# An own PSUM tile for product six's seed in the first block of units of an FNet and FFN kernel, and some 300 pieces in another order

## The chip, the cores and the metric

The kernel runs on one core of a Trainium2 chip. The metric is the device time of one execution in microseconds (us). The kernel before took 670.1 us (median of three runs, 669.82 to 670.17).

## What is computed

A Fourier mixing layer with a residual, then a feed-forward layer with a residual, on 2048 rows of 512 numbers:

```python
def _A_ref(x, dft_seq_re, dft_seq_im, dft_hid_re, dft_hid_im):
    a = jnp.einsum("bsd,ed->bse", x, dft_hid_re)
    b = jnp.einsum("bsd,ed->bse", x, dft_hid_im)
    return jnp.einsum("ts,bse->bte", dft_seq_re, a) - jnp.einsum("ts,bse->bte", dft_seq_im, b)
...
def _B_ref(x, w1, w2):
    return silu(x @ w1) @ w2          # w1 512 x 1792, w2 1792 x 512
...
h = x + _A_ref(_layernorm(x), ...)
h2 = h + _B_ref(_layernorm(h), w1, w2)
```

## The kernel before

**Matmuls.** Every number that goes into a matmul is split in two parts, a rounded one (names that end in `h`) and the remainder (names that end in `l`). ScalarE (ACT) writes the rounded part, VectorE (DVE) the remainder: for most pieces these are the lines L265 and L269 (L271 where the sign changes), with the parts called `ph` and `pl`. One product of two such pieces is three matmuls on TensorE (PE), written by `three` at L313 to L317: rounded by rounded (L315), weight's rounded part by the other's remainder (L316), and weight's remainder by the other's rounded part (L317). So a matmul on L316 is the first that needs a new `pl`.

**Stages.** The rows are cut in two halves, q = 0 and q = 1. The order on PE is: `plain(0, 0)`, `fast(1, 0)`, `mix_fast(0)` (the Fourier layer for the first half of the columns of the spectrum), `fast(0, 1)`, `fast(1, 1)`, `mix_fast(1)` (the other half), then `up(0)` with the first part of `down(0)` inside it, the rest of `down(0)`, `up(1)` with the first part of `down(1)` inside, and the rest of `down(1)`. `fast`, `mix_fast`, `up` and `down` form block products by seven products in place of eight, so that sums and differences of blocks have to be made on DVE (L713 sums of DFT blocks `raw`, L834 sums of `c` and `h` blocks, L1141 to L1144 sums of the blocks `u` and `v` of w2, L1154 remainders of these, `Ul` and `Vl`). `h` blocks with the residual are made by L834 from the banks `y` that `mix_fast(1)` leaves.

**`up`.** `up(q)` multiplies the normed rows, as seven blocks T1 to T7, by w1. The hidden units come in seven blocks of 256, p = 0 to 6. The products of a block have numbers. For p = 0 they stand in the order 1, 7, 6, 2, 5; for the others in the order 1, 7, 3 (of the block ahead), 6, 2, 4 (of the block ahead), 5. Each product is six matmuls of 128x512. Three PSUM buffers of a block collect them: Y takes the products 1, 6, 5 and 3, V takes 7 and 4, and X takes 2. X doesn't start at zero but with product one: after it, `post(1)` has ACT copy Y to X at L1082. This copy is called the seed here. Product six goes on adding into Y, so it must wait until the seed has read product one out of Y. That is the seed of the title.

**Tiles.** PSUM is a pool of four tiles of two banks each (`banks`, L259). `mm` at L1061 takes a tile for Y at product one, and at product seven a tile whose first bank is V and whose second bank is X (L1065, L1066). A wait is set between whole tiles: an instruction that writes a tile waits for the last instructions that wrote or read that tile, on either bank. The names in the profile are those of the tiles: `y` for Y, `vx` for V and X.

**What sets the order.** `program` doesn't issue anything at once. It makes a list of events, each with a time in us, a class and a function: `step` (L321) makes the matmuls of a product, what has to be ready ahead of them (so long ahead) and what follows (so long behind). At the end the list is sorted by time plus `MOVED[number]` (table at L48 to L155: a number of us by which an event is moved). The launch replays the sorted list, and `issue_after` keeps each engine's instructions in that order. So the order of each of the five queues (PE, DVE, ACT, GpSimd as POOL, SyncE as SP) comes from these times. The same sorted list also sets which of 51 SBUF pages every block gets (`Plan`), and so which earlier reader a write to a page waits for. A seed's event stands at the end of product one plus `SEED_US`, 0.05 (L1127 in `up`), and since the events of product seven have the time of that end, the seed is recorded behind product seven.

Of the kernel before, what the change touches and what calls it, by code (L numbers as in the profile page):

```python
# [51 lines left out]
    31: -141.11, 32: -134, 33: -264.77, 34: -169.45, 35: -126.48, 36: -103.37, 37: -217.84, 38: -155.57, 39: -94.89,  # L52
    40: -79.42, 41: -142.14, 42: -135.16, 44: -117.87, 45: -98.55, 46: -92.57, 48: -183.29, 49: -129.46, 50: -108.53,
    52: -98.47, 53: -97.74, 54: -16.55, 56: -4.92, 57: -23.81, 58: -8.89, 59: -147.46, 60: -133.99, 61: -101.4,
    62: -14.81, 63: -139.64, 64: -134.82, 65: -9.83, 66: -7.55, 67: -130.2, 68: -99.62, 69: -129.85, 71: -159.25,
    72: -134.4, 73: -167.67, 74: -112.4, 75: -90, 76: -8.28, 78: -130.86, 79: -106.36, 80: -186.23, 81: -152.86,
    82: -111.9, 84: -114.65, 85: -104.21, 86: -113.16, 87: -95.06, 88: -11.303, 89: -19.86, 92: -21.38, 93: -18.33,
    94: -129.79, 95: -106.07, 96: -6.71, 97: 1.06, 98: -97.01, 99: -91.41, 100: -17.37, 102: -27.59, 103: -16.9,
    104: -102.24, 106: -1.27, 107: -9.08, 108: -204.21, 109: -106.59, 110: -253.17, 111: -121.9, 112: -39.16,
    114: -2.55, 115: 0.78, 116: 3.06, 118: -49.98, 119: -21.09, 121: -8.78, 122: -3.61, 123: 2.24, 125: 1.31,  # L60
    126: -17.83, 127: -3.73, 129: 0.38, 130: 1.11, 132: -7.91, 133: 0.36, 135: 0.25, 136: -1.05, 138: -3.38,
    139: -40.3, 140: -33.76, 142: -9.61, 143: -11.31, 145: -2.69, 146: -10.66, 147: -10.63, 148: -8.83, 149: -7.82,
    150: -3.56, 151: -28.92, 152: 0.89, 153: 5.11, 154: 28.43, 155: 25.79, 156: -19.1, 157: 11.48, 158: 12.64,
    159: 23.23, 160: 21.61, 161: -6.36, 162: -4.7, 163: -3.36, 164: 0.29, 165: -2.68, 166: -0.5, 167: -0.32,
    168: -3.05, 169: -6.02, 170: -7.36, 171: -16.72, 172: -14.58, 173: -1.38, 174: -3.55, 175: -6.71, 176: -1.18,
    177: 6.42, 178: 2.55, 179: 3.85, 180: 2.57, 181: -55.12, 182: -141.38, 183: -35.06, 184: -35.03, 185: -33.65,
    186: -22.94, 187: -27.65, 188: -24.62, 189: -15.8, 190: -18.21, 191: -20.38, 192: -17.85, 193: -18.3, 194: -16.61,
    195: -16.49, 196: -37.35, 197: -39.52, 198: -8.42, 199: -16.79, 200: -18.96, 201: -10.89, 202: -33.77,
    203: -23.77, 204: -6.04, 205: -22.6, 206: -26.07, 207: -19.3, 208: -13.56, 209: -11.57, 210: -2.02, 211: -14.92,
    212: -13.44, 213: -2.69, 214: -12.02, 215: -4.58, 216: -5.05, 217: -7.76, 218: -5.18, 219: 4.31, 220: -26.78,  # L70
    221: -14.68, 222: 2.53, 223: -1.3, 224: 9.8, 225: 9.6, 226: -4.61, 227: -6.71, 228: 7.13, 229: -6.57, 230: 4.19,
    231: 2.3, 233: -17.54, 234: -3.28, 235: -2.51, 237: -5.35, 238: 3.96, 239: 1.79, 241: -16.85, 242: -8.31,
    243: -10.48, 245: 2.48, 246: -6.71, 247: 5.57, 248: 4.96, 250: -7.84, 251: 4.88, 252: 7.47, 254: -3.03,
    255: -1.83, 256: -3.76, 258: -3.74, 259: -1.52, 260: 0.28, 262: 14.24, 263: -3.6, 264: 6.12, 265: 4.15,
    267: -1.21, 268: 1.61, 269: 1.26, 271: -12.23, 272: 6.33, 273: 4.4, 275: 6.84, 276: 3.77, 277: 4.66, 279: 8.32,
    280: 2.16, 281: 3.8, 282: -2.2, 283: -3.37, 284: 3.13, 285: -5.36, 287: 2.19, 288: 7.38, 290: 1.75, 291: 0.99,
    293: 7.28, 294: 5.11, 295: -0.57, 296: 2.29, 297: 1.12, 298: -6.11, 300: 6.15, 301: 5.36, 302: 6.99, 304: 0.33,
    305: 0.04, 307: 4.4, 308: 5.67, 310: 6.65, 311: 6.52, 312: 4.54, 313: 6.14, 314: 6.33, 315: 2.16, 317: 4.42,
    318: 5.39, 319: 6.85, 321: -1.92, 322: 0.78, 324: 7.21, 325: 5.83, 327: 5.44, 328: 3.63, 329: 5.68, 330: 5.23,
    331: 4.54, 332: 3.57, 335: 5.77, 336: 6.96, 337: 7.55, 339: 1.8, 340: 7.4, 343: 1.08, 344: 2.71, 347: 5.46,  # L80
    348: 7.81, 349: 7.74, 352: -11.6, 353: -5.61, 354: 0.23, 355: 7.05, 356: 4.21, 359: 4.35, 362: 0.73, 363: 3.66,
    364: -18.86, 366: 2.5, 367: 4.06, 371: -3.02, 372: 2.17, 374: 11.59, 376: 2.43, 377: 2.49, 380: 4.33, 381: 19.37,
    382: 4.31, 383: 5.86, 385: 0.07, 391: 3, 392: 5.29, 393: 4.78, 394: 5.84, 396: -6.06, 398: 3.97, 399: 5.33,
    402: 4.7, 403: 2.54, 404: 1.44, 407: 4.06, 408: 4.25, 411: 3.24, 412: 3.09, 413: 4.05, 414: 5.92, 417: 5.6,
    418: 6.69, 420: 16.42, 422: 4.72, 423: 5.68, 424: 0.95, 425: 4.17, 428: 5.12, 429: 3.15, 430: -5.26, 432: 13.47,
    433: 30.5, 434: -12.86, 435: -18.34, 436: -20.06, 437: -17.24, 438: -20.28, 439: -14.87, 440: -17.12, 441: -18.08,
    442: -8.62, 443: -3.41, 444: 6.22, 445: 4.67, 446: 4.65, 447: 3.36, 448: -30.45, 449: -29.1, 450: -35.51,
    451: -21.41, 452: -16.94, 453: -18.24, 454: -12.602, 455: -15.99, 456: -8.99, 457: -10.56, 458: 1.51, 459: -5.57,
# [1300 lines left out]
```

## Time and profile before

| | before |
|---|---|
| median of three runs | 670.1 us (669.82 to 670.17) |
| the profiled execution's own time | 670.99 us |
| its span, first to last instruction | 669.2 us |
| granted TensorE clock, mean | 0.999 |
| PE busy | 659.8 us, 99% |
| DVE busy | 578.3 us, 86% |
| ACT busy | 369.5 us, 55% |
| POOL busy | 97.1 us, 15% |
| DMA, mean of the span | 275 GB/s |

Times in the profile are us from the first instruction. A row of the timeline has the start, the duration, the engine, the line, the operation, what it writes and reads, and in square brackets how long the engine sat idle ahead of it and what released it. `PEld` rows are weight loads, which run beside matmuls. A matmul's recorded duration is 0.39 us, but they are pipelined: in a row of matmuls without a wait one starts about 0.227 us behind the other. A DVE operation also overlaps the next a little: 128x1024 takes 1.22 us in its row, and the next starts 1.13 to 1.14 us behind it.

### The profile page before, as it was taken

To read this page: it belongs to the slowest core of one execution; us is meant where nothing else is said; L and a number is where in the kernel's file an instruction comes from. 1 tells how busy PE (TensorE), PEld (TensorE's weight loads), DVE (VectorE), ACT (ScalarE), POOL (GpSimd) and SP (SyncE) were. 2 spreads that over 40 slices of the span, in tenths; PEclk is the share of its full clock that TensorE was granted. 3 is DMA by queue.
4 is the path that set the end of the run, shared out by engine and by line. 5 is a ranking of instruction groups with operands and counts; after the bars stand their busy time and mean duration, and the time that the engine had idled before them with its cause. 6 is when DMAs were issued, how large, how long until landed. Compare 5 with 4: busy or idle time off the path is not lost. (4 is left out here: it accounts for less than half of the span.)

```text
span 669.2 us, 8292 instructions
## 1 busy us (share of the span) xinstructions
PE 659.8 (99%) x2892; PEld 541.6 (81%) x2892; DVE 578.3 (86%) x727; ACT 369.5 (55%) x476; POOL 97.1 (15%) x128
## 2 busy tenths in 40 slices
PE   9999999999999999999999999999999999999997
PEld 5888888888888888887878878888888788888885
DVE  7999978998989989989999998989998854369964
ACT  6996546754465336455656445778544555664600
POOL 0011011112002523211120015243000000000000
PEclk9999999999999999999999999999999999999999
DMA  8973899798996768999999993859989635278803
GB/s 316 375 190 81 263 332 417 233 329 262 385 361 259 242 215 198 389 296 377 359 332 414 334 401 120 328 214 321 343 278 361 232 116 221 79 248 310 322 31 127
DMA packets 59706, 184.22 MB, mean 275 GB/s; under 512 B 6800, under 2 KB 13840, under 8 KB 59664
## 3 DMA queue, kind: packets, MB, share of 16 engines
q1 hardware_dynamic: 45456, 132.79, 55.5%
q0 software_dynamic: 13920, 50.63, 23.6%
q8 instruction: 23, 0.38, 0.2%
q10 hardware_dynamic: 288, 0.26, 0.1%
q14 instruction: 19, 0.16, 0.1%
HBM read 139.34 MB, written 44.32 MB: 274 GB/s over the span
## 5 line engine op out<-in xcount | busy, mean ns | idle before, releaser
L265 ACT ACTIVATE ph<-raw 128x1024 fp32r<-128x1024 f32 x102 | 105.7, 1055 | 81.1 <-PE m L317 19.3
L269 DVE TENSOR_TENSOR pl<-raw,ph 128x1024 fp32r<-128x1024 f32 x88 | 111.4, 1288 | 6.0 <-ACT ph L265 4.3
L315 PE MATMUL m<-ph,S 128*128 128x512 f32 x192 | 74.7, 389 | 0.0
L316 PE MATMUL m<-pl,S 128*128 128x512 f32 x192 | 74.7, 389 | 0.0
L317 PE MATMUL m<-ph,S 128*128 128x512 f32 x192 | 74.7, 389 | 0.0
L315 PE MATMUL f<-gth,wf 128*128 128x512 f32 x161 | 62.6, 389 | 0.0
L317 PE MATMUL f<-gth,wf 128*128 128x512 f32 x161 | 62.6, 389 | 0.0
L316 PE MATMUL f<-gtl,wf 128*128 128x512 f32 x161 | 62.6, 389 | 0.0
L265 ACT ACTIVATE gth<-g 128x1024 fp32r<-128x1024 f32 x42 | 42.6, 1053 | 31.7 <-DVE g L1203 30.7
L316 PE MATMUL m<-pl,X 128*128 128x512 f32 x144 | 56.4, 392 | 1.4 <-DVE pl L269 1.4
L269 DVE TENSOR_TENSOR gtl<-g,gth 128x1024 fp32r<-128x1024 f32 x42 | 50.2, 1218 | 6.8 <-ACT gth L265 5.5
L317 PE MATMUL m<-ph,X 128*128 128x512 f32 x144 | 56.1, 389 | 0.0
L315 PE MATMUL m<-ph,X 128*128 128x512 f32 x144 | 56.0, 389 | 0.0
L713 DVE TENSOR_TENSOR raw<-raw,raw 128x1024 f32<-128x1024 f32 x36 | 45.7, 1273 | 1.0 <-DMA raw<-in_seq 0.4
L1076 DVE TENSOR_TENSOR g<-vx,g 128x512 f32<-128x512 f32 x28 | 19.3, 689 | 30.4 <-PE vx L317 16.6
L316 PE MATMUL y<-pl,hf 128*128 128x512 f32 x112 | 43.6, 389 | 0.0
L315 PE MATMUL y<-ph,hf 128*128 128x512 f32 x112 | 43.6, 389 | 0.0
L317 PE MATMUL y<-ph,hf 128*128 128x512 f32 x112 | 43.6, 389 | 0.0
L315 PEld LDWEIGHTS m<-ph,S 128*128 128x128 f32 x192 | 36.1, 188 | 7.5
L316 PEld LDWEIGHTS m<-pl,S 128*128 128x128 f32 x192 | 36.0, 188 | 7.5
L317 PEld LDWEIGHTS m<-ph,S 128*128 128x128 f32 x192 | 36.0, 188 | 7.4
L316 PEld LDWEIGHTS f<-gtl,wf 128*128 128x128 f32 x161 | 30.2, 188 | 6.3
(399 smaller groups left out, 1539.4 us busy)
## 6 DMA issues: line engine op xcount, KB each, us to landing
raw<-in_seq SPq DMA_DIRECT2D x84, 512.0 KB, 6.6
hf<-fd SPq DMA_DIRECT2D x28, 512.0 KB, 7.5
wf<-wd SPq DMA_DIRECT2D x28, 512.0 KB, 5.7
wf<-wd SPq DMA_DIRECT2D x28, 384.0 KB, 5.6
sf<-sd SPq DMA_DIRECT2D x18, 512.0 KB, 7.2
raw<-in_seq POOLq DMA_DIRECT2D x16, 512.0 KB, 7.0
fd<-hf POOLq DMA_DIRECT2D x14, 512.0 KB, 7.1
w<-in_ffn SPq DMA_DIRECT2D x23, 256.0 KB, 5.9
```

Of the source, the lines that this page charges most:

```text
L265: nc.scalar.activation(hi, src, AF.Copy, scale=sign)
L269: nc.vector.tensor_tensor(lo, src, hi, op=ALU.subtract)
L315: nc.tensor.matmul(acc, wh, mh, start=first, stop=False, skip_group_check=on)
L316: nc.tensor.matmul(acc, wh, ml, start=False, stop=False, skip_group_check=on)
L317: nc.tensor.matmul(acc, wl, mh, start=False, stop=last, skip_group_check=on)
L713: nc.vector.tensor_tensor(o, a, b, op=ALU.subtract)
L1076: nc.vector.tensor_tensor(g[q, f][:, tau, :], src, g[q, f][:, tau, :], op=ALU.add)
```

## The change

For the first block of units (p = 0, in both halves) X gets a PSUM tile of its own, called `x`, taken in `post(1)` when the seed is recorded; the tile of product seven then holds V alone (its second bank stays empty there). The seed's event stands right at the end of product one, without the 0.05, and is recorded ahead of product seven. For p from 1 to 6 nothing changes in this. So the pool gives out 76 tiles in place of 74.

Beside that, 254 entries of the table `MOVED` have other values, nearly all by more than 1 us, so that some 300 instructions stand elsewhere in the queues of DVE, ACT, POOL and SP, and blocks get other pages. The order of PE's matmuls stays as it was. Line numbers above 155 are higher by one in the changed kernel, and from L1069 on by up to five (the seed is L1087 there, `rounded`'s remainder L270, the matmuls L316 to L318).

```diff
-    114: -2.55, 115: 0.78, 116: 3.06, 118: -49.98, 119: -21.09, 121: -8.78, 122: -3.61, 123: 2.24, 125: 1.31,
+    114: -2.55, 115: 0.78, 116: 3.06, 118: -8.45, 119: -4.96, 121: -8.78, 122: -3.61, 123: 2.24, 125: 1.31,
...
             if n == 7:
                 t = banks(f"vx{q}{p}")
-                bank[p, "V"], bank[p, "X"] = t[:, 0, :], t[:, 1, :]
+                bank[p, "V"] = t[:, 0, :]
+                if p:
+                    bank[p, "X"] = t[:, 1, :]
             mul(n, p, n in (1, 7), n in (2, 6, 5, 3, 4))
...
             if n == 1:
                 for i in range(2):
                     g[q, 2 * p + i] = page(f"g{q}{p}{i}")
+                if not p:
+                    bank[p, "X"] = banks(f"x{q}{p}")[:, 0, :]
                 nc.scalar.activation(bank[p, "X"], bank[p, "Y"], AF.Copy)
...
-            after = [(SEED_US if n == 1 else 0, lambda n=n, p=p: post(n, p))]
+            after = [(SEED_US if n == 1 and p else 0, lambda n=n, p=p: post(n, p))]
```

The first place is ACT's queue at the start of `up(0)`. In the names, `y00` is the tile Y of half 0 and block 0, `vx00` that of V and X, `x00` the new one; `wah` is the rounded part of w1, `T2h` and `T6h` that of the normed rows, `Uh` and `Vh` that of w2's blocks, and `g` the block of activated units. In square brackets stand the engines and DMA queues whose semaphore the instruction waits for. Before:

```order
L1045 ACTIVATE wah00_3385<-w1_3200 128x768 [waits DMAHW4_49,DMAHW3_49,DVE_49]
L265 ACTIVATE T2h_3418<-hn010_2872 128x1024 [waits PE_49]
L1153 ACTIVATE Uh_3422<-u4_3165 128x768 [waits DMAHW6_49,DMAHW3_49,PE_49]
L265 ACTIVATE T6h_3425<-hn011_2929 128x1024 [waits DVE_49]
L1045 ACTIVATE wah01_3450<-w1_3364 128x768 [waits DMAHW5_49,DMAHW4_49,PE_49]
L1082 ACTIVATE vx00_3466<-y00_3455 128x512 [waits PE_49]
L1073 ACTIVATE g001_3474<-y00_3455 128x512 [waits PE_49,DVE_49,Activation_49,Pool_49]
```

After:

```order
L266 ACTIVATE ph_3412<-c2211_3114 128x1024 [waits PE_49]
L1158 ACTIVATE Uh_3416<-u4_3166 128x768
L266 ACTIVATE T6h_3419<-hn011_2922 128x1024 [waits DVE_49,PE_49]
L1046 ACTIVATE wah01_3444<-w1_3358 128x768 [waits DMAHW2_49,DMAHW1_49,PE_49]
L1087 ACTIVATE x00_3459<-y00_3449 128x512 [waits DVE_49,PE_49]
L1076 ACTIVATE g001_3458<-y00_3449 128x512 [waits PE_49,Activation_49]
```

The seed stands at the same place in ACT's queue, behind `wah01`. Its wait for PE is for another matmul: before for product seven's last, since it writes the tile that product seven writes, now for product one's last. The new tile also makes it wait for DVE, for the last reader of the two banks it gets (the sum that makes `h101` from bank `y17`), and product seven's first matmul waits for the last reader of the banks that `vx00` gets (the sum that makes `h100` from `y12`).

The second place is DVE's queue near 300 us, in `fast(1, 1)`. `raw11310` is a DFT block (its digits: c, q, the block's row jj, then k and tau), and `u1`, `v1` are blocks of w2. Before:

```order
L269 TENSOR_TENSOR pl_2584<-raw11210_2471,ph_2583 128x1024 [waits DMAHW3_49,DMASW3_49,Activation_49]
L713 TENSOR_TENSOR raw11301_2530<-raw11311_2534,raw11301_2530 128x1024 [waits DMAHW0_49,DVE_49]
L271 SCALAR_TENSOR_TENSOR pl_2646<-raw11211_2364,ph_2645 128x1024 [waits PE_49,Activation_49]
L1141 TENSOR_TENSOR v1_2577<-u1_2576,v1_2577 128x256 [waits DMAHW3_49,DMAHW1_49]
L1142 TENSOR_TENSOR v1_2577<-u1_2576 128x256 [waits DMAHW2_49]
L1143 TENSOR_TENSOR v1_2577<-v1_2577,u1_2576 128x256 [waits DVE_49]
L1144 TENSOR_TENSOR u1_2576<-u1_2576,v1_2577 128x256 [waits DVE_49]
L269 TENSOR_TENSOR pl_2666<-raw11310_2512,ph_2665 128x1024 [waits DMAHW5_49,Activation_49]
```

After:

```order
L272 SCALAR_TENSOR_TENSOR pl_2571<-raw11211_2362,ph_2570 128x1024 [waits Activation_49]
L270 TENSOR_TENSOR pl_2575<-raw11011_2466,ph_2574 128x1024 [waits DMASW7_49,DMAHW2_49,DVE_49,Activation_49]
L270 TENSOR_TENSOR pl_2578<-raw11111_2451,ph_2577 128x1024 [waits DMAHW1_49,PE_49,Activation_49]
L714 TENSOR_TENSOR raw11300_2545<-raw11301_2543,raw11300_2545 128x1024 [waits DMAHW7_49,DMAHW6_49]
L270 TENSOR_TENSOR pl_2581<-raw11210_2468,ph_2580 128x1024 [waits DMAHW3_49,Activation_49]
L714 TENSOR_TENSOR raw11301_2543<-raw11311_2547,raw11301_2543 128x1024 [waits DMAHW0_49,DMASW0_49,DVE_49]
L270 TENSOR_TENSOR pl_2528<-raw11200_2360,ph_2527 128x1024
L270 TENSOR_TENSOR pl_2631<-raw11310_2525,ph_2630 128x1024 [waits DMAHW5_49,DVE_49,Activation_49]
```

The four sums of `u1` and `v1` are gone from the place ahead of `pl` of `raw11310` and stand 25 rows further on; `pl` of `raw11211` stands five pieces earlier, ahead of `pl` of `raw11011`, and `pl` of `raw11200`, which stood 13 rows ahead of `pl` of `raw11310` before, now stands right ahead of it.

The third place is DVE's queue some 40 rows on, near 345 us. Before:

```order
L1154 TENSOR_TENSOR Ul_2932<-u1_2576,Uh_2931 128x768
L408 TENSOR_TENSOR wal02_3015<-w1_2971,wah02_3014 128x768 [waits DMAHW4_49,DMAHW3_49,Activation_49]
L269 TENSOR_TENSOR pl_2952<-c12_2828,ph_2951 128x1024 [waits DMAHW6_49,DMASW4_49,DMASW0_49]
L269 TENSOR_TENSOR pl_3025<-raw11011_2627,ph_3024 128x1024 [waits DMASW6_49,DVE_49,Activation_49]
L834 TENSOR_TENSOR c12_2828<-c12_2828,c11_2755 128x1024 [waits DVE_49]
```

After:

```order
L1159 TENSOR_TENSOR Ul_2925<-u1_2668,Uh_2924 128x768
L1159 TENSOR_TENSOR Ul_2998<-u2_2781,Uh_2997 128x768 [waits Activation_49]
L270 TENSOR_TENSOR pl_2948<-c12_2826,ph_2947 128x1024 [waits DMAHW6_49]
L270 TENSOR_TENSOR pl_3020<-raw11011_2624,ph_3019 128x1024 [waits DMASW6_49,PE_49,Activation_49]
L835 TENSOR_TENSOR c12_2826<-c12_2826,c11_2754 128x1024 [waits DVE_49]
L1159 TENSOR_TENSOR Vl_3027<-v2_2782,Vh_3026 128x1024 [waits Activation_49]
L1159 TENSOR_TENSOR Vl_2968<-v1_2669,Vh_2967 128x1024 [waits DMASW3_49]
```

`wal02`, the remainder of a block of w1, is gone from here (it stands 19 rows behind `pl` of `raw11011` now), `Ul` of `u2` came in in its place, and `Vl` of `v1`, which stood 28 rows ahead of `pl` of `raw11011` before, stands three rows behind it.

201 rows, old and new, of the table MOVED are left out of this document.

## The prediction

> **What bounds the kernel now.** I read the busy shares on the profile's page first, then the list of what PE waited for, and then the timeline around each of those waits. The page says that PE is the bound nearly everywhere:
>
> ```profile
> span 669.2 us, 8292 instructions
> PE 659.8 (99%) x2892; PEld 541.6 (81%) x2892; DVE 578.3 (86%) x727; ACT 369.5 (55%) x476; POOL 97.1 (15%) x128
> ```
>
> The order of the matmuls doesn't change, so their 659.8 us stay. The change can only take out, or put in, time in which PE waits for something. What it waits for now is this list (engine, operation and line that waited; what it waited for; us in total, times, longest):
>
> ```profile
> PE y L315 <- ACT vx L1082: 1.7, 2, 1.0
> PE m L316 <- DVE pl L269: 1.4, 2, 1.0
> PE idle L1352 <- DVE upper L1345: 1.2, 1, 1.2
> PE c L516 <- DVE X L408: 0.4, 1, 0.4
> ```
>
> So the two seeds (L1082) and two late remainders `pl` cost PE something; the last two rows lie in the start-up. No DMA is on the list. These totals count from the recorded end of the matmul ahead, which is 0.39 us long though the next could start after about 0.227, so I price each wait by its starts, from the timeline. Here is the seed of the first half:
>
> ```profile
> 396.51 0.39 PE L317 MATMUL y<-T1h,wal 128*128 128x512 f32 x1
> 396.74 0.39 PE L315 MATMUL vx<-T7h,sf 128*128 128x512 f32 x1
> 397.87 0.39 PE L317 MATMUL vx<-T7h,sf 128*128 128x512 f32 x1
> 398.30 0.58 ACT L1082 ACTIVATE vx<-y 128x512 f32<-128x512 f32 x1 [3.00 <-PE vx L317]
> 398.93 0.50 PE L315 MATMUL y<-T6h,sf 128*128 128x512 f32 x1 [0.67 <-ACT vx L1082]
> ```
>
> Product one's last matmul starts at 396.51, product seven's six go from 396.74 to 397.87 (1.13 over five steps: 0.226 each), and only when the last of them has ended, at 398.26, does ACT copy, though it had sat idle for 3.00 us and product one had ended at 396.90. Product six was due one step behind product seven, at 398.10, and starts at 398.93: 0.83 lost, and 0.11 more since its first matmul takes 0.50 in place of 0.39. That is 0.94 us. The second half has the same picture:
>
> ```profile
> 529.84 1.03 ACT L1222 ACTIVATE p<-f 128x1024 f32<-128x1024 f32 x1 [1.19 <-PE f L317]
> 530.78 0.39 PE L317 MATMUL y<-T1h,wal 128*128 128x512 f32 x1
> 532.14 0.39 PE L317 MATMUL vx<-T7h,sf 128*128 128x512 f32 x1
> 532.90 0.58 ACT L1082 ACTIVATE vx<-y 128x512 f32<-128x512 f32 x1 [2.03 <-PE vx L317]
> 533.54 0.50 PE L315 MATMUL y<-T6h,sf 128*128 128x512 f32 x1 [1.01 <-ACT vx L1082]
> ```
>
> Due at 532.14 + 0.226 = 532.37, started at 533.54, with the same 0.11: 1.28 us. Here the seed began 0.37 behind the end of product seven (532.53), in the first half 0.04 behind it. The two seeds cost 2.22 us together.
>
> Now the two waits for `pl`, DVE's rows and PE's:
>
> ```profile
> 301.67 0.42 DVE L1141 TENSOR_TENSOR v<-u,v 128x256 f32<-128x256 f32 x1
> 303.14 1.22 DVE L269 TENSOR_TENSOR pl<-raw,ph 128x1024 fp32r<-128x1024 f32 x1
> 303.56 0.39 PE L315 MATMUL m<-ph,X 128*128 128x512 f32 x1
> 304.41 0.50 PE L316 MATMUL m<-pl,X 128*128 128x512 f32 x1 [0.46 <-DVE pl L269]
> ```
>
> ```profile
> 343.23 0.95 DVE L408 TENSOR_TENSOR wal<-w,wah 128x768 fp32r<-128x768 f32 x1
> 344.10 1.22 DVE L269 TENSOR_TENSOR pl<-c,ph 128x1024 fp32r<-128x1024 f32 x1
> 345.16 0.39 PE L315 MATMUL m<-ph,X 128*128 128x512 f32 x1
> 345.23 1.22 DVE L269 TENSOR_TENSOR pl<-raw,ph 128x1024 fp32r<-128x1024 f32 x1
> 346.50 0.50 PE L316 MATMUL m<-pl,X 128*128 128x512 f32 x1 [0.96 <-DVE pl L269]
> ```
>
> At 303.56 + 0.23 = 303.79 the second matmul was due and started at 304.41: 0.62 and 0.11 for the longer one, 0.73 us. At 345.39 it was due and started at 346.50: 1.11 and 0.11, 1.22 us. In both DVE hands out `pl` late because it is full of work, with the four sums of `u1` and `v1` in front (303.14 − 301.67 = 1.47 us) and with `wal` (0.87 to the next start).
>
> All four waits together are 2.22 + 0.73 + 1.22 = 4.17 us. That is the most that the change can take out of PE's queue behind the start-up.
>
> **The change part by part.** *The own tile.* With it the seed waits for product one, which ends at 396.90, and starts at the latest as far behind that as it stood behind product seven in the two rows, 0.04 to 0.37 us: 396.94 to 397.27. It takes 0.58, the next engine answers some 0.05 later (398.88 to 398.93), so product six could start at 397.57 to 397.90, and is due at 398.10. In the second half product one ends at 530.78 + 0.39 = 531.17, ACT has ended its copy at 530.87, the seed ends at 531.79 to 532.12, and product six is due at 532.37: 0.2 to 0.5 to spare. What hides the seed is product seven's 1.36 us; if ACT were busy with one more 128x1024 piece (1.03) when product one ends, most of the wait would be back. The order has no such piece in the first half, where `wah01` stands ahead of the seed as before, and ACT sat idle before both seeds (3.00 and 2.03). Gain 2.22, with a lower bound of 0.9 should the second half's seed be held up. No row of before shows a seed beside product seven's matmuls; the other seeds, of p from 1 on, stand behind product seven as well. The copy by itself can't lose time, since it waits for an earlier matmul than before.
>
> The tile's price is the wait for other banks. `x00` waits for DVE's sum from bank `y17`, `vx00` for DVE's sum from `y12`, both pieces of the residual of `mix_fast(1)`. Whether they are done is a matter of DVE's load. It is full there (busy us of PE, PEld, DVE, ACT, POOL, with counts; clock, DMA share, GB/s):
>
> ```profile
> 240.00:286.00 46.00, 46.00 (x204) 38.03 (x204) 44.08 (x46) 21.44 (x23) 10.57 (x11) 1.00 0.81 250
> 346.50:395.00 48.50, 48.50 (x214) 40.17 (x215) 48.36 (x49) 26.17 (x29) 6.42 (x12) 1.00 1.02 388
> ```
>
> From 346.5 to 395 DVE has 0.14 us to spare in 48.5. In the order after, 37 pieces of 128x1024, five of 128x768 and two groups of four sums stand behind `pl` of `raw11011` up to and with the sum from `y12`. At 1.135, 0.87 and 1.47 us (steps of the rows above) they take 42.0 + 4.35 + 2.94 = 49.3 us. If that `pl` starts 1.13 earlier than at 345.23 (next part), the sum from `y12` is read at about 344.10 + 1.13 + 49.3 + 0.1 = 394.6. Product seven needs it at 396.74 less the 1.95 us that PE gains at the two `pl` places, so at 394.8 (395.0 with the 0.2 that I leave at 345, below). Two tenths of a microsecond are left; I cost it at nothing, and at up to 1 us as the other end, by the two waits of DVE quoted next.
>
> *The place at 303.* The sums of `u1` and `v1` go behind, `pl` of `raw11211` five pieces ahead. `pl` of `raw11310` is then done at least 1.47 earlier than 304.36, at 302.9, and due at 303.79. Gain 0.73, with 0.9 to spare.
>
> *The place at 345.* Ahead of `pl` of `raw11011` now go `Ul` of `u2` in place of `wal02` (0.87 each), and `Vl` of `v1` has gone behind it. Its row and two later waits of DVE:
>
> ```profile
> 319.03 1.22 DVE L1154 TENSOR_TENSOR Vl<-v,Vh 128x1024 fp32r<-128x1024 f32 x1
> ...
> 325.04 1.23 DVE L1154 TENSOR_TENSOR Vl<-v,Vh 128x1024 fp32r<-128x1024 f32 x1 [0.52 <-ACT Vh L1153]
> 326.93 1.23 DVE L271 SCALAR_TENSOR_TENSOR pl<-raw,ph 128x1024 fp32r<-128x1024 f32 x1 [0.67 <-ACT ph L265]
> ```
>
> That is 1.13 less, so `pl` ends at 346.45 − 1.13 = 345.32, while PE, which has gained 0.73 at 303, comes at 345.39 − 0.73 = 344.66: 0.71 late, with 0.11 on top. Against that DVE's wait of 0.67 at 326.93 should go: the rounded part that it waits for stands seven rows earlier in ACT's queue. So the rest of the wait lies between 0 and 0.82, and I take 0.2, near the lower end, since the 0.67 has a row of its own. Gain 1.0.
>
> *The other moved pieces.* Most stand in DVE's queue at places where PE doesn't wait. Three put more ahead of a remainder that PE needs soon, and the room that they have is in these rows:
>
> ```profile
> 241.23 1.29 DVE L920 SCALAR_TENSOR_TENSOR hr<-m,h 128x512 f32<-128x512 f32 x2 [2.44 <-PE m L317]
> ...
> 258.81 2.35 DVE L269 TENSOR_TENSOR pl<-raw,ph 128x1024 fp32r<-128x1024 f32 x2
> ```
>
> ```profile
> 260.25 0.40 PE L316 MATMUL m<-pl,S 128*128 128x512 f32 x1
> ...
> 284.75 0.39 PE L316 MATMUL m<-pl,X 128*128 128x512 f32 x1
> ```
>
> At 260 the two `pl` of the x2 row change places: the one that PE needs at 260.25 ended at 260.03 and would end at 261.16, 0.9 late. At 284.75 a `pl` (1.13) and six small operations of a root come ahead, about 2.2 us against 0.8 to spare; at 287.5 one piece against 1.2. Taken alone these are waits of 0.9, 1.4 and none. But DVE's 2.44 us of idling ahead of 241.23 is filled with pieces from behind (`pl` of `raw01311` and of `raw01211`, the sum into `hr010`), so that DVE reaches all three places up to 2.4 us earlier. Some of that is lost again where a piece then waits for ACT or a load; by hand each place keeps about 0.4 us. I take 0.5 us for all of them and for moved loads, an estimate; its ends are 0 (all hidden) and 2.3 (none, 0.9 + 1.4).
>
> One thing can stretch DVE's pieces (min, median, max in ns):
>
> ```profile
> L269 DVE TENSOR_TENSOR pl<-raw,ph x88: 1207/1217/3264, 15.7 to 352.4; 128x1024 fp32r<-128x1024 f32 x88
> ```
>
> ```profile
> L905 POOL PARTITION_ALL_REDUCE v<-v x4: 3228/3608/4132, 220.6 to 453.3; - x4
> ```
>
> A `pl` is 1.22 us, and 3.26 where one of POOL's eight reductions over partitions runs beside it, 2.05 more. The number of reductions stays, so in sum DVE loses what it lost; only which piece is hit changes. The Trainium skill, "SBUF — State Buffer", section "Who interferes with whom", has a rule for that: a DVE instruction with two SBUF inputs contends with a GpSimd instruction that reads SBUF, and it is an exclusive lock rather than a sharing. By that rule the sum above stays as it is, unless a hit falls on a piece that PE waits for; the trace, with 3264 against a median of 1217, agrees. No matmul takes part in it.
>
> *Loads.* Some 90 rows of SP's and POOL's queues differ. PE waited for no DMA before, and a load that comes late would cost PE its lateness; I have it in the 0.5.
>
> Sum: 2.22 + 0.73 + 1.0 − 0.5 = 3.45 us. The profiled execution took 670.99 us with a span of 669.2, so it would take 667.5; against the median of 670.1 that is 666.6 us.
>
> **The rivals.** *What PE gains ahead of 395 it gives back there.* DVE has no idle time from 346.5 to 395. If its waits for ACT don't go, or a stretched piece falls in, the sum from `y12` (or `pl`, or T6's remainder) comes up to 2 us later than PE wants it, and PE waits at product seven for what it gained at 303 and 345. Then only the seeds pay: 670.1 − 2.22 = 667.9. For it speaks the margin of 0.2 us, against it that most of the 1.95 us comes from work taken out ahead. Chance 0.25.
>
> *New waits inside `fast(0, 1)` and `fast(1, 1)`.* If the 2.44 us of idling isn't filled (its cause, PE's product for `hr`, holds back others in the queue), the waits of 0.9 and 1.4 come at 260 and 284.75, and by the later clock the seeds and the two places still pay: 670.1 − 4.17 + 0.2 + 2.3 = 668.4, and near 669.0 with one more wait for a load of half a microsecond. Chance 0.12.
>
> *Slower: stretched remainders.* The reductions now stand beside other pieces. Where a piece that is needed within 0.4 us is stretched by 2.05, PE waits about 1.65, and DVE, busy 44.08 of 46.00 us and 48.36 of 48.50 in the two windows above, doesn't catch up soon. Four such hits of the eight would be 6.6 us against the 4.17: 670.1 + 6.6 − 4.2 = 672.5. The kernel is slower than before from the third hit on (5.0 against 4.2), and by more than can be told apart from the fourth. For it speaks the 3264 ns row, against it that before PE waited for no stretched piece (both `pl` that it waited for took 1.22). The same rule of the Trainium skill, in "SBUF — State Buffer", "Who interferes with whom", would give this outcome its cause. Chance 0.06.
>
> *The change doesn't do what it says.* If the seed still waited for product seven, the gain would be 0.73 + 1.0 − 0.5 = 1.2 us, 668.9. The order's waits speak against it: a tile of its own, recorded ahead of product seven. Chance 0.02.
>
> **How the numbers follow.** My forecast, between 665.8 and 667.4, has 0.55, and the time is its value, 666.65, given as 666.6 us. The lower end of the range, 665.7, is 670.1 − 4.17 and two tenths for what measurement leaves open. The upper end takes in the first two rivals, 667.9 and 668.4 with 669.0, so 669.0. A measurement of this kernel can tell about 0.2%, 1.34 us, from no change: faster is below 668.76, slower above 671.44. Forecast and first rival, 0.55 + 0.25, are faster: 0.80. The second rival lies at the bound, and the fourth within 0.2%: 0.12 + 0.02, of which I give 0.01 to a worse case of the second, so 0.13 for the same. Slower has 0.07: the 0.06 of the stretched pieces and that 0.01.
>
> **What would show it.** In the changed kernel's list of PE's waits the row for the seed should be gone, with the seeds at about 0.05 to 0.4 us behind product one's end and ACT's copy beside product seven's matmuls. No wait for `pl` should stand near 303; one of at most 0.8 near 344.5. DVE should be busy ahead of 241. Wrong would be: a PE wait for DVE's `h` or T6 near 395 (the first rival), for `pl` near 260 or 285 (the second), a `pl` of over 3 us right ahead of a wait (the third), for a DMA anywhere (then my 0.5 is mis-sized).

## The result and the profile after

The changed kernel takes 666.39 us (median of four runs, 666.04 to 666.84) against 670.13 (669.82 to 670.18) for the kernel before: 3.74 us less, a ratio of 0.9946 with the interval 0.9928 to 0.9963. The forecast was 666.6 in a range from 665.7 to 669.0. The profiled execution took 666.04 us with a span of 664.2, against 670.99 and 669.2. In the experiments below a few executions took 739 to 2382 us; they are left out of every median, and where the profiled one was among them (two kernels) its PE waits aren't read.

The first thing to read is the page's span and busy times, and the list of what PE waited for:

```profile
span 664.2 us, 8287 instructions
PE 657.6 (99%) x2892; PEld 541.8 (82%) x2892; DVE 575.7 (87%) x727; ACT 371.6 (56%) x476; POOL 97.8 (15%) x128
```

```profile
PE idle L1357 <- DVE upper L1350: 1.2, 1, 1.2
PE c L513 <- DVE X L489: 0.5, 1, 0.5
```

Both rows that are left lie in the start-up. Behind it PE waits for nothing: from matmul to matmul there is no step over 0.245 us. Before, such steps made up 4.32 us: 0.94, 1.29, 0.73, 1.23, and 0.13 at 115.9 that the forecast had left out. Of the rest of the 5.0 us between the two spans, 0.7, 0.52 lies in the first 10 us of the two executions, and the remainder in single steps of PE that were a few hundredths longer than usual. The medians differ by 3.74.

The first half's seed, PE's and ACT's rows (to be read beside those of 396 to 399 before):

```profile
393.71 0.39 PE L318 MATMUL y<-T1h,wal 128*128 128x512 f32 x1
...
394.13 0.58 ACT L1087 ACTIVATE x<-y 128x512 f32<-128x512 f32 x1 [3.23 <-PE y L318]
...
395.07 0.39 PE L318 MATMUL vx<-T7h,sf 128*128 128x512 f32 x1
...
395.30 0.39 PE L316 MATMUL y<-T6h,sf 128*128 128x512 f32 x1
```

The copy now starts 0.03 behind product one's end (393.71 + 0.39 = 394.10), ends at 394.71, and product six follows product seven at its usual step, 395.30 − 395.07 = 0.23. The releaser in ACT's row is `y`, product one, and no longer `vx`. In the second half:

```profile
526.08 1.03 ACT L1227 ACTIVATE p<-f 128x1024 f32<-128x1024 f32 x1 [1.20 <-PE f L318]
...
527.01 0.39 PE L318 MATMUL y<-T1h,wal 128*128 128x512 f32 x1
...
527.50 0.58 ACT L1087 ACTIVATE x<-y 128x512 f32<-128x512 f32 x1 [0.39 <-PE y L318]
...
528.60 0.39 PE L316 MATMUL y<-T6h,sf 128*128 128x512 f32 x1
```

The copy starts 0.10 behind product one's end (527.40), and ends 0.52 ahead of product six.

The two places of `pl`, DVE's rows and PE's matmul that needs it (the second piece of the x2 row is `pl` of `raw11310`, at 303.14 before; 340.35 and 341.48 answer to 344.10 and 345.23 before):

```profile
297.33 2.53 DVE L270 TENSOR_TENSOR pl<-raw,ph 128x1024 fp32r<-128x1024 f32 x2
...
340.35 1.22 DVE L270 TENSOR_TENSOR pl<-c,ph 128x1024 fp32r<-128x1024 f32 x1
341.48 1.22 DVE L270 TENSOR_TENSOR pl<-raw,ph 128x1024 fp32r<-128x1024 f32 x1
```

```profile
303.04 0.39 PE L317 MATMUL m<-pl,X 128*128 128x512 f32 x1
...
343.84 0.39 PE L317 MATMUL m<-pl,X 128*128 128x512 f32 x1
```

`pl` of `raw11011` is done at 342.70, 1.14 ahead of the matmul at 343.84. `pl` of `raw11310` is done at 299.86, 3.2 ahead of 303.04. DVE's share of the two windows (before first, then after; behind the window's length stand the busy times of PE, of its weight loads and of DVE):

```profile
304.00:346.50 42.50, 41.13 (x180) 33.70 (x180) 40.73 (x48) 26.24 (x31) 8.08 (x13) 1.00 1.03 347
```

```profile
304.00:346.50 42.50, 42.50 (x189) 35.21 (x188) 42.29 (x48) 26.41 (x30) 7.11 (x12) 1.00 1.01 340
346.50:395.00 48.50, 48.50 (x215) 40.16 (x215) 47.88 (x49) 25.20 (x29) 5.78 (x11) 1.00 1.00 394
```

DVE had 1.77 us of idling from 304 to 346.5 before and has 0.21 after; both of its waits for ACT (0.52 and 0.67) are gone. That isn't where the room at 345 comes from, though, since the windows don't hold the same pieces. From the start of `pl` of `raw11310` to that of `pl` of `raw11011` DVE took 42.09 us before (303.14 to 345.23) and takes 42.84 after (298.64 to 341.48): its idling in between went from 1.76 to 0.98, but four sums, a `pl` and an `Ul` came in for `wal` and a `Vl`. So the second `pl` starts 3.75 us earlier because the first starts 4.50 earlier, and the room at 345 was made ahead of 303. And the price of the new tiles isn't paid: the sum from `y12` that product seven's banks wait for ends at 391.66 + 1.22 = 392.88, and product seven starts at 393.94.

```profile
391.66 1.22 DVE L835 TENSOR_TENSOR h<-y,h 128x1024 f32<-128x1024 f32 x1
...
393.94 0.39 PE L316 MATMUL vx<-T7h,sf 128*128 128x512 f32 x1
```

### The profile page after: what moved, and what is told of

It is laid out like the page before. It is cut to its first block, busy times and chain, and to the rows that moved or that the text cites. A ratio compares the mean times of both kernels' runs of the same rounds, so it can differ in the third digit from the quotient of the medians.

```text
span 664.2 us, 8287 instructions
## 1 busy us (share of the span) xinstructions
PE 657.6 (99%) x2892; PEld 541.8 (82%) x2892; DVE 575.7 (87%) x727; ACT 371.6 (56%) x476; POOL 97.8 (15%) x128
## 4 chain that ended last, share of the span: by engine, by line
PE 98%; DMA 0%; DVE 0%; ACT 0%; issue 0%; DVEq 0%
PE m L317 11%; PE m L316 11%; PE m L318 11%; PE y L316 8%; PE y L318 8%; PE y L317 8%; PE f L318 6%; PE f L316 6%; PE f L317 6%; PE c L317 4%; PE c L318 4%; PE c L316 4%; PE vx L316 3%; PE vx L318 3%; PE vx L317 3%; PE c L517 1%
## 5 line engine op out<-in xcount | busy, mean ns | idle before, releaser
L270 DVE TENSOR_TENSOR pl<-raw,ph 128x1024 fp32r<-128x1024 f32 x88 | 112.1, 1289 | 9.1 <-ACT ph L266 7.1
L316 PE MATMUL m<-ph,S 128*128 128x512 f32 x192 | 74.7, 389 | 0.0
L318 PE MATMUL m<-ph,S 128*128 128x512 f32 x192 | 74.7, 389 | 0.0
L316 PE MATMUL f<-gth,wf 128*128 128x512 f32 x161 | 62.6, 389 | 0.0
L318 PE MATMUL f<-gth,wf 128*128 128x512 f32 x161 | 62.6, 389 | 0.0
L270 DVE TENSOR_TENSOR gtl<-g,gth 128x1024 fp32r<-128x1024 f32 x42 | 50.3, 1219 | 7.0 <-ACT gth L266 5.7
L316 PE MATMUL m<-ph,X 128*128 128x512 f32 x144 | 56.0, 389 | 0.0
L318 PE MATMUL m<-ph,X 128*128 128x512 f32 x144 | 56.0, 389 | 0.0
L714 DVE TENSOR_TENSOR raw<-raw,raw 128x1024 f32<-128x1024 f32 x36 | 43.9, 1221 | 0.5
L316 PE MATMUL y<-ph,hf 128*128 128x512 f32 x112 | 43.6, 389 | 0.0
L318 PE MATMUL y<-ph,hf 128*128 128x512 f32 x112 | 43.6, 389 | 0.0
L316 PEld LDWEIGHTS m<-ph,S 128*128 128x128 f32 x192 | 36.0, 188 | 7.5
L318 PEld LDWEIGHTS m<-ph,S 128*128 128x128 f32 x192 | 36.0, 188 | 7.5
```

Source lines behind the costliest of these rows:

```text
L270: nc.vector.tensor_tensor(lo, src, hi, op=ALU.subtract)
L316: nc.tensor.matmul(acc, wh, mh, start=first, stop=False, skip_group_check=on)
L318: nc.tensor.matmul(acc, wl, mh, start=False, stop=last, skip_group_check=on)
L714: nc.vector.tensor_tensor(o, a, b, op=ALU.subtract)
```

## The experiments

The theory: four waits of PE paid, each with its own length; the seeds through the tile, the `pl` places through DVE's order. The main rivals: the tile and the moved pieces pay only together, or the place right behind product one is what pays rather than the tile. Each run was timed beside the kernel before on its own chip, and each difference below is to that.

**Tile or order.** The tile of its own with the table as before, timed twice:

```diff
 (the changed kernel's code, with MOVED as before)
```

> The kernel before with the tile of its own alone, the order of pieces as before. My theory: the tile pays only with the moved residual. In the old order the sum that makes h101 from bank y17 stands at 401.3 us, and the new tile gets that bank, so the first half's seed can copy only at 402.6 and product six starts at about 403.2 in place of 398.1: 5.2 us lost where 0.94 were lost before; the second half gains its 1.28. In all 670.1 + 5.2 - 0.94 - 1.28 = 673.1 us. The rival, that the tile pays by itself whatever the order: 670.1 - 2.22 = 667.9 us.

Measured: 668.77 against 670.59 (ratio 0.9979, 0.9966 to 0.9992), 1.8 us faster by the medians and 1.4 by the ratio, and not 3 slower. My theory of what the tile needs fell. The waits are read from the second time:

> The kernel before with the tile of its own alone once more, for a trace at the full clock. What I gave out for it, a loss of 3 us, rested on the new tile getting the bank of y17. In the old order the pool gives it the bank of y12, read long before, and V gets that of y11. My theory now: no seed waits; product seven waits for the sum that makes h110 from y11, which ended at 396.8 before and is due at 396.75: 0.1 us and 0.1 for the slower matmul. With the waits at 303 and 345 as before, 670.1 - 2.22 + 0.2 = 668.1 us on the chip of before, about 2 us less than the kernel before beside it. The rival, that the old reason stands: PE waits 5 us at product six, 3 us more than before.

Measured: 668.13 against 670.52 (0.9958, 0.9945 to 0.9972), 2.4 us faster. PE's list and the rows at the seed:

```profile
PE m L316 <- DVE pl L269: 1.3, 2, 0.9
PE idle L1356 <- DVE upper L1349: 1.2, 1, 1.2
```

```profile
394.86 1.23 DVE L834 TENSOR_TENSOR h<-y,h 128x1024 f32<-128x1024 f32 x1 [0.36 <-PE y L317]
...
395.79 0.39 PE L317 MATMUL y<-T1h,wal 128*128 128x512 f32 x1
...
396.14 0.50 PE L315 MATMUL vx<-T7h,sf 128*128 128x512 f32 x1
396.22 0.58 ACT L1086 ACTIVATE x<-y 128x512 f32<-128x512 f32 x1 [0.73 <-PE y L317]
```

No seed is on the list. What the tile costs alone is at product seven: the sum from `y11` ends at 396.09, and the matmul starts at 396.14, not at 396.02: 0.12, and 0.11 for the longer one. The first expectation took it that the new tile gets the banks of `y17` in any order. In this one the sum from `y17` is recorded later than the tile is taken. The rows agree with this second expectation, by which the pool gave `x00` the banks of `y12` and `vx00` those of `y11`: product seven waits for the sum that ends at 396.09, and the seed for product one alone.

With the one sum from `y17` moved as in the change as well:

```diff
+MOVED.update({782: 5.37})          # h101 <- y17
```

> The same, and of all the moved pieces one alone: the sum that makes h101 from y17 stands some ten rows earlier in DVE's queue, as in the change. My theory: both seeds pay in full, 670.1 - 2.22 = 667.9 us, and the waits at 303 and 345 stay (0.73 and 1.22). The rival, that DVE, full at that place, then hands the remainder of T6 or the sum for h110 over too late: at least 1 us of it comes back near 398, 669 us or more.

Measured: 668.79 against 670.59 (0.9972, 0.9958 to 0.9986), 1.8 less. The trace has no wait near 397. What is left behind the start-up are waits for `pl` (this list is this kernel's; its two places are 115.8 and 346.8):

```profile
PE m L317 <- DVE pl L270: 2.1, 2, 1.9
```

By its starts the wait at 303 was 0.27 here, with the longer matmul, and the one at 345 was 2.17; in the trace above they were 0.63 and 1.17, and before 0.73 and 1.23. So the two aren't fixed while the order is the old one. The runs spread from 667.46 to 671.41, and the three slowest of the twelve (670.68 and more) show a mean granted clock of 0.997, the others 0.999 or 1.000.

The moved pieces without the tile:

```diff
 (the kernel before, with MOVED as in the change)
```

> The other way round: all moved pieces, X and V in one tile as before. My theory: the places at 303 and 345 pay, 1.95 us, and the seeds cost their 2.22 as before: 668.2 us, or 666.4 + 2.2 = 668.6 from the other side. The rival, that the moved pieces only help the tile: 670 us.

Measured: 668.68 against 670.59 (0.9970, 0.9959 to 0.9981), 1.91 less, in a spread of 0.7. Only the seeds are left behind the start-up:

```profile
PE y L316 <- ACT vx L1083: 1.4, 2, 0.7
```

They cost 0.94 and 1.00. Tile and order each give about half: 1.8 to 2.4 and 1.9, together 3.7 to 4.3, with 4.20 for both in the run with the late seed below.

**Tile or place.** The changed kernel with X and V in one tile again, taken at the seed, so that the seed stands ahead of product seven:

```diff
             if n == 1:
...
                 if not p:
-                    bank[p, "X"] = banks(f"x{q}{p}")[:, 0, :]
+                    t = banks(f"vx{q}{p}")
+                    bank[p, "V"], bank[p, "X"] = t[:, 0, :], t[:, 1, :]
```

> The changed kernel, but for the first block X and V share one tile again, which is taken at the seed, so the seed is recorded ahead of product seven. My theory: the wait is by tile, so now product seven waits for the seed: it ends 0.58 + 0.04 behind product one's end, and PE loses about 0.8 + 0.1 us in the first half and 0.9 + 0.1 in the second: 668.3 us, nothing gained over the old place. The rival, that the place right behind product one is what pays: 666.4 us.

Measured: 668.55 against 670.59 (0.9971, 0.9959 to 0.9982), as much as the order alone.

```profile
394.08 0.39 PE L318 MATMUL y<-T1h,wal 128*128 128x512 f32 x1
...
394.50 0.58 ACT L1086 ACTIVATE vx<-y 128x512 f32<-128x512 f32 x1 [3.23 <-PE y L318]
395.14 0.50 PE L316 MATMUL vx<-T7h,sf 128*128 128x512 f32 x1 [0.67 <-ACT vx L1086]
```

The seed is as early as in the changed kernel, 0.03 behind product one's end, and now product seven waits for it: due at 394.31, started at 395.14. The wait has only moved from product six to product seven.

And the tile with the seed recorded behind product seven:

```diff
-            after = [(SEED_US if n == 1 and p else 0, lambda n=n, p=p: post(n, p))]
+            after = [(SEED_US if n == 1 else 0, lambda n=n, p=p: post(n, p))]
```

> The changed kernel, with the tile of its own but the seed recorded behind product seven as before (the 0.05 kept). My theory: only the tile decides, since the queues of PE and ACT are apart and the seed waits for product one's semaphore either way: 666.4 us, no wait at the seeds. The rival, that it has to be recorded ahead of product seven: 668.6 us.

Measured: 666.28 against 670.48 (0.9938, 0.9926 to 0.9950), 4.20 less. The seed's place in the list is worth nothing; the tile of its own is what pays. The one wait behind the start-up, at 284, is 0.16 with 0.11 behind it, where the changed kernel's margin was 0.33.

**How much is hidden.** The seed three times in a row:

```diff
-                nc.scalar.activation(bank[p, "X"], bank[p, "Y"], AF.Copy)
+                for _ in range(1 if p else 3):
+                    nc.scalar.activation(bank[p, "X"], bank[p, "Y"], AF.Copy)
```

> The changed kernel with the seed's copy done three times in a row in the first block, to measure what product seven hides. By the trace after the change one seed leaves 0.53 us before product six in the first half and 0.47 in the second; two copies more take about 0.96. My theory: PE waits 0.42 and 0.49 us and 0.11 more each, 1.1 us: 667.5 us. The rival, that more is hidden (the copies overlap, or product six is held by something else): 666.4 us.

Measured: 667.99 against 670.48 (0.9965, 0.9953 to 0.9977), and 1.71 more than the run before, timed beside it.

```profile
394.22 1.81 ACT L1088 ACTIVATE x<-y 128x512 f32<-128x512 f32 x3 [3.23 <-PE y L318]
```

```profile
395.16 0.39 PE L318 MATMUL vx<-T7h,sf 128*128 128x512 f32 x1
396.08 0.50 PE L316 MATMUL y<-T6h,sf 128*128 128x512 f32 x1 [0.54 <-ACT x L1088]
```

Three copies into the same place take 1.81, 0.61 a step and not the 0.48 that I had taken. Product six is due at 395.38 and starts at 396.08: 0.70, and 0.76 in the second half, with 0.11 each: 1.68. One seed leaves 0.5 us, the upper end of what the forecast had; by these steps a second, 0.61 behind the first, would have missed its time by about 0.1.

**DVE's order.** The sums of `u1`, `v1` back ahead of `pl` of `raw11310`, with their loads:

```diff
+MOVED.update({829: -10.88, 830: -13.96})
```

> The changed kernel with the four sums of u1 and v1, and their loads, back ahead of pl of raw11310. By the trace after the change that pl is done 3.2 us early, and the sums take 1.47. My theory: the sums themselves are covered, but they wait for their load, which landed at 301.0 before; DVE stands still until then, and pl is done at about 303.7 against 302.9: a wait of 0.8 and 0.1, 667.3 us. The rival, that the 3.2 us cover it: 666.4 us.

Measured: 668.02 against 670.48 (0.9962, 0.9949 to 0.9975), 1.74 over the run with the late seed.

```profile
298.26 1.23 DVE L271 TENSOR_TENSOR pl<-raw,ph 128x1024 fp32r<-128x1024 f32 x1 [2.34 <-ACT ph L267]
...
301.68 0.42 DVE L1147 TENSOR_TENSOR v<-u,v 128x256 f32<-128x256 f32 x1
...
303.14 1.22 DVE L271 TENSOR_TENSOR pl<-raw,ph 128x1024 fp32r<-128x1024 f32 x1
```

```profile
304.42 0.50 PE L318 MATMUL m<-pl,X 128*128 128x512 f32 x1 [0.88 <-DVE pl L271]
...
310.56 0.50 PE L318 MATMUL m<-pl,X 128*128 128x512 f32 x1 [0.41 <-DVE pl L271]
```

DVE's rows stand to a hundredth where they stood before the change, and the wait is back: 1.04 with 0.11, and a second of 0.57 with 0.11 at 310. But it isn't the load that holds DVE up, as I had expected: it sat idle for 2.34 us ahead of 298.26, for a rounded part of ACT, and was full from there on. So the sums cost PE what they cost before only once DVE is late, and the room of 3.2 us goes as soon as a rounded part comes late. Why that part is late shows in ACT's rows, of this kernel and of the changed one:

```profile
297.10 1.06 ACT L267 ACTIVATE ph<-raw 128x1024 fp32r<-128x1024 f32 x1 [3.57 <-DMA v<-in_ffn]
```

```profile
294.99 1.06 ACT L266 ACTIVATE ph<-raw 128x1024 fp32r<-128x1024 f32 x1 [0.57 <-DMA cd<-u]
```

The load that the first row names lands only at 300.8. By the times it is the same store of a block `u` (`cd<-u`) that ends the longer part of the wait: issued at 288.29, it landed at 296.75, after 8.5 us, in the changed kernel after 7.0. Two of the moved loads, of `u`, are issued here at 287.84 and 288.27, right ahead of that store, where the changed kernel issues none. That they slow it down is likely and not shown.

`wal02` and `Vl` of `v1` back ahead of `pl` of `raw11011`:

```diff
+MOVED.update({932: -57.73, 933: -58.13, 934: -57.09, 834: 22.44})   # round and remainder of w1, sums, Vl
```

> The changed kernel with wal02 and Vl of v1 (2.0 us together) back ahead of pl of raw11011. By the trace after the change that pl is done 1.14 us ahead of its matmul. My theory: 2.0 - 1.14 + 0.05 = 0.9 us of waiting there and 0.1 for the slower matmul, 667.4 us. The rival, that DVE's waits for ACT ahead of it take it up: 666.4 us.

Measured: 672.82 against 670.48 (1.0036, 1.0024 to 1.0049), 6.5 over the run with the late seed. Far more than 0.9, and by another way than either theory (ACT's row, PE's, and a window of 5 us):

```profile
343.29 0.85 ACT L1047 ACTIVATE wah<-w 128x768 fp32r<-128x768 f32 x1 [4.80 <-DMA w<-in_ffn]
```

```profile
346.08 0.51 PE L317 MATMUL m<-ph,X 128*128 128x512 f32 x1 [2.17 <-ACT ph L267]
348.32 0.79 PE L318 MATMUL m<-pl,X 128*128 128x512 f32 x1 [1.74 <-DVE pl L271]
348.91 0.63 PE L319 MATMUL m<-ph,X 128*128 128x512 f32 x1
```

```profile
349.00:354.00 5.00, 5.00 (x13) 3.87 (x12) 4.96 (x8) 1.59 (x2) 1.06 (x2) 0.50 1.02 420
```

The rounding of w1 (`wah`) has to stand ahead of the remainder, and it waits 4.80 us for a load that lands at 343.18 here and landed at 340.05 before; behind it in ACT's queue stand the rounded parts that PE needs, and PE waits 2.33 and 2.01 us with one matmul between. Then its granted clock is 0.50 for 5 us and a matmul comes every 0.427 us. One of the eight executions, the only one at a mean clock of 0.999 and not 0.994 to 0.997, took 670.52, 4.2 over the run with the late seed: about what the two waits are without the slow matmuls. The experiment shows what a piece costs that goes ahead of its load, not what the 1.14 us of room are worth.

Three pieces of DVE back where they stood near 240 us:

```diff
+MOVED.update({527: 6.94, 534: 6.11, 449: -29.1})   # pl of raw01311 and raw01211, sum into hr010
```

> The changed kernel with three pieces of DVE's queue back where they stood near 240 us (pl of raw01311 and raw01211 and the sum into hr010, behind the sum into hr011 that waits for PE). My theory: DVE sits idle there for about 2.4 us again, and since after the change the remainders at 260, 284 and 287 are done only 0.86, 0.33 and 0.43 us ahead of their matmuls, PE waits at one or two of them, 1.0 to 2.3 us in all: about 668.0 us. The rival, that other idle time of DVE takes it up: 666.4 us.

Measured: 671.50 against 670.49 (1.0014, 1.0004 to 1.0023), slower than before.

```profile
243.37 1.29 DVE L922 SCALAR_TENSOR_TENSOR hr<-m,h 128x512 f32<-128x512 f32 x2 [4.50 <-PE m L319]
244.58 1.22 DVE L273 SCALAR_TENSOR_TENSOR pl<-raw,ph 128x1024 fp32r<-128x1024 f32 x1
```

```profile
245.86 0.50 PE L318 MATMUL m<-pl,S 128*128 128x512 f32 x1 [2.37 <-DVE pl L273]
```

DVE idles 4.50 us ahead of the sum into `hr011`, more than the 2.44 of before. The remainder behind that wait is late at once (2.53 with 0.11), and the waits that the forecast feared come too, 1.16 with 0.11 at 262 and 0.33 with 0.11 at 288: 4.35 in all.

But this isn't the wait of before. The operation that writes `hr` (`center` in the kernel) reads `h` and POOL's mean (the `m` in its row), and no product of PE. What it can wait for of PE is the last matmul that read the page it is given, and the pages follow the order. Before, the wait ended with the first of these two matmuls, here with the second:

```profile
240.73 0.39 PE L317 MATMUL m<-ph,S 128*128 128x512 f32 x1
```

```profile
242.88 0.39 PE L319 MATMUL m<-ph,S 128*128 128x512 f32 x1
```

In PE's order the second stands 12 matmuls, 2.7 us, behind the first (which stands at 240.16 here). Had DVE waited for the first one, the remainder at 244.58 would have been done at 243.1, ahead of its matmul, which was due at 243.33 (an estimate from these rows). So the 4.35 us are the price of this order with its pages, and not that of the three pieces.

Two chains alone in the old order, and all moves up to 340 us alone:

```diff
 (the kernel before)
+MOVED.update({829: -0.17, 830: 13.62, 833: 18.5, 834: 25.77, 835: 22.3})   # w2 block 1
+MOVED.update({932: -49.2, 933: -42.89, 934: -47.15, 935: -36.24, 936: -36.11})   # w1 block 2
```

> The kernel before, with two chains of pieces moved as in the change and nothing else: the loads, sums, rounding and stores of u1 and v1, and the rounding, remainder and sums of the w1 block whose remainder is wal02. If these pieces are what the places at 303 and 345 wait for, as the sum in the prediction has it, both waits go: 670.1 - 1.95 = 668.2 us. My theory by now: 303 goes (0.73), but the sums come in ahead of 345 and DVE waits for ACT in between, so that the wait there grows from 1.2 to about 1.8 us: 669.9 us. The wait at 345 then needs the other moves.

```diff
 (the kernel before with the tile, and MOVED as in the change for 782 and the 196 events ahead of 340 us)
```

> The tile of its own, the moved sum from y17, and of the other moved pieces only those that stand ahead of 340 us in both lists (196 of 254); the 57 behind stand as before. My theory: what pays behind the start-up is the seeds and DVE's queue ahead of 345; pl of raw11011 keeps about 1.1 us to spare, since wal02 stays ahead of it but the remainder of u2 doesn't come in. So no wait behind the start-up: 666.3 us, as the changed kernel. The rival, that the pieces behind 340 are needed as well (two chains alone in the old order brought a wait for a load near 380): 0.8 us or more behind 346, 667.2 us.

Measured: 672.66 against 670.49 (1.0030, 1.0018 to 1.0042), and 671.93 against 670.52 (1.0028, 1.0016 to 1.0040): both are slower than before. In the first the wait at 303 is gone as its expectation has it, but DVE waits for a load of a DFT block, and PE waits in new places, for DVE at 334 and 337 (0.38 and 0.62) and near 380 for a load of `hf` (0.85), while the 1.28 at 345 stay:

```profile
316.96 2.36 DVE L714 TENSOR_TENSOR raw<-raw,raw 128x1024 f32<-128x1024 f32 x2 [5.89 <-DMA raw<-in_seq]
```

```profile
PE y L316 <- ACT vx L1083: 1.7, 2, 1.0
PE m L317 <- DVE pl L270: 1.6, 3, 1.0
...
PE y L316 <- DMA hf<-fd: 0.6, 1, 0.6
```

In the second, whose waits of PE aren't read, ACT's `wah` again waits 4.9 us for w1's load, as in the run with `wal02` back, whose place it shares. All five executions behind the median show a mean granted clock of 0.996, as seven of the eight of that run do (0.994 to 0.997). That this wait is the cause is likely and not shown.

## Why the prediction was right

**The seeds (2.22).** Right in size and cause. The waits of 0.94 and 1.29 are gone, the tile alone brings 1.8 and 2.4 in its two runs, with 0.23 of new waiting in the trace, and the earlier place isn't needed. The margins of 0.2 to 0.5 were 0.53 and 0.47 in the changed kernel's trace, counted as in the forecast with 0.05 for the answer. The bank wait that I costed at nothing with two tenths to spare had 1.06 to spare, but that was luck. From the start of `pl` of `raw11011` to the end of the sum from `y12` DVE took 51.40 us (341.48 to 392.88, 0.61 of it idling) and not my 50.53. From the 344.10 at which I let that `pl` start, the sum would have ended at 395.5, half a microsecond behind the 395.0 at which I needed it. It held because DVE was there 2.6 us earlier than I had it.

**303 (0.73).** The wait is gone, and comes back with the sums (1.04 and 0.11). The room was larger than the 0.9 of the sum, 3.2, since `pl` started 4.50 earlier and not only by the 1.47 of the sums. Of the rest, 0.7 is that all of PE's work there stands so much earlier, and 2.3 come from the order ahead of it, which I haven't followed piece by piece.

**345 (1.0 of 1.22).** The whole 1.23 went, with 1.14 to spare; the sum had 0.71 left over, and set 0.2 for it. The term was mis-sized because I reckoned it from DVE's rows near 345 alone, 1.13 less in front and one wait of 0.67 gone, with DVE otherwise where it was. The wait did go, but between the two places DVE took 0.75 us longer than before, not less. The room is what was left of the 4.50 us by which DVE was early at 303, a term that the sum doesn't have. What moves made it is not settled: the pieces named alone, in the old order, leave the wait at 345 where it was, but there a late load confounds them.

**The allowance (−0.5).** No wait came at 260, 284 or 287, nor for a load: this term is 0 in the trace of the changed kernel. DVE's 2.44 us of idling ahead of 241.23 are gone, as the forecast had it, but their cause was misread: it was a page that PE still read, and no product of PE. The term isn't empty, though. The margins at the three places are 0.86, 0.33 and 0.43, near the 0.4 that I had, and in a near copy of the kernel 284 cost 0.27. The far end of 2.3 wasn't measured: the 4.35 with three pieces put back at 240 has another, later page in it, and with it the remainder right behind that wait, which I had left out.

Put together the trace lost 4.32 us of waits where the forecast took 3.45; the four-run median gained 3.74, and the near copy 4.20 with an interval of 0.9926 to 0.9950 that covers both. That the time came within 0.2 us of the forecast is therefore partly luck: the terms alone were 0.87 too small in the trace. Against the first rival (what is gained at 303 and 345 is given back at 395) speaks the order alone, which brings 1.9. The second rival, new waits inside `fast`, came only with the three pieces put back, and from a longer wait than it had. Stretched remainders cost nothing: no `pl` of 3 us stands ahead of a wait of PE.

## What to carry to other kernels

If a wait is tracked by tile, look at what shares the tile before moving an instruction: here the seed's earlier place was worth nothing without a tile of its own, and the tile everything without the place. Where the order also sets which page a block gets, a piece that is put back doesn't put the old wait back: the three pieces at 240 us met a later reader of their page, and the kernel was slower than before. Read what made the room for a piece from where the engine stands when it gets there, and not from its idling in a window near by. And don't move a piece ahead of what it has to wait for: on a queue kept in order the wait is passed to all that stands behind.

## What the runs showed of the hardware

After two waits of 2.33 and 2.01 us with a single matmul between them PE's granted clock fell to 0.50 for about 5 us, and its matmuls came every 0.427 us in place of 0.227: some 14 steps, 2.9 us on top of the waits. In the profiled execution of another kernel (the three pieces back) the matmuls behind a single wait of 2.53 us came at the usual step. Its mean granted clock was 1.000, though, and seven of the ten executions of that kernel show 0.995 to 0.997 and 671.37 to 671.99 us, the other three 670.60 to 671.17; no trace shows where those seven lost their clock. The Trainium skill, "TensorE: Matmul & The Clock Gate", in "Part 1: The HAM clock gate (the "warmup" mystery)", has half the clock after an idle window of some 3.4 us. The two waits together, 4.3 us, agree with that if one matmul between doesn't break the window, and so does the profiled 2.53 alone; the seven executions leave it open, and no run here shows where the line lies.

Three kernels in the new order (the late seed, the order alone, the shared tile) agree among their runs to 0.2 to 0.9 us (666.11 to 666.33, 668.34 to 669.04, 668.27 to 669.16); the runs of the one with the old order and one moved piece lie up to 4 apart (667.46 to 671.41). The late `pl` at 345 cost 1.23, 1.17, 2.17 and 1.28 in the traces of four kernels with it.
